# Sigmoid attention into a SwiGLU block on one Trainium2 core: gate and val of the last two batches by seven block products after attention, with weight sums kept in DRAM

## The chip, the core and the metric

The kernel runs on one core of a Trainium2 chip. The metric is the device time of one execution in microseconds (us); of several executions the median is given.

## The reference

Attention with a sigmoid in place of the softmax, and then a feed-forward block with a gated activation. The output of attention, with its heads put side by side, is the feed-forward block's input.

```python
scores = q @ k.T / sqrt(64) - log(448)      # per batch and head: 8 batches, 12 heads, 448 tokens, head size 64
attn   = sigmoid(scores) @ v
x      = attn, heads side by side           # 3584 tokens x 768
g      = x @ w_gate                         # 768 x 1536
out    = (g * sigmoid(g) * (x @ w_val)) @ w_out   # 1536 x 768, float32
```

## The kernel before, in words

**Attention.** One step `i` takes four heads of one batch; three steps make a batch, so there are NQ = 24 steps. SyncE loads q, k and v (`load`, L291), GpSimd casts them (`cast_qk`, `cast_v`), a DMA transpose makes q and k head-size-major (`tr_dma`, L406), TensorE multiplies the scores (`burst`, L417), ScalarE takes the sigmoid (`sig`, L443, tiles `pt`, a ring of 10), TensorE multiplies with v (`pv`, L455), and DVE and ScalarE copy the result out of PSUM as fp16 tiles `xT` (six per batch, 128 model features x 448 tokens, a ring of 14).

**Gate and val, called F1 here.** `f1` (L529) takes one batch and two of the 12 blocks of 128 hidden columns. Gate is 2 x 6 products of 128x128 weights with 448 tokens. Each product is made of four 64x64 quarter matmuls, which run at the same time in four parts of the array (`quarters`, L511, the matmul is L522). ScalarE takes the sigmoid of the gate (L546), DVE multiplies it with the gate out of PSUM (L552), then val follows in the same way and DVE multiplies the two (L559) into `hT`, the hidden tile of a pair of batches.

**The output product, called F2 here.** For two token tiles of 128 `f2_set` (L631) splits the hidden features and the output columns in halves and makes the product with seven block products in place of eight (the Winograd form of Strassen's method). `weight_sums` (L594) makes the four sums of w_out's blocks once, on DVE, and keeps them in staging slots that are free by then (`wsum`, L244). Each set needs sums of hidden tiles on DVE (L661, L664, L667, L734) and sums of results out of PSUM (L687). Two products are issued together as quarters (`f2_pair`, L757, at L522 too); single ones are full-array matmuls (`f2_single`, L788, at L678), which all of the last pair of batches are.

**The order of the work** comes from a planner in the kernel (`list_schedule`, L70). The code from L868 on appends operations, step by step, with a duration, what they depend on, and which buffers they take and give back; the planner goes through time and lets each engine start, out of a window of the next 30 to 40 of its operations, the first one that is ready. The result is a fixed order for each engine's queue; on the chip each engine runs its queue in that order. In before, F1 follows attention at one block per quarter of a step (`LAG`), F2 is added at a rate of 12.5/22 pairs per quarter step, and what is left goes behind. The stores of F2 results are issued on GpSimd's queue during attention and on SyncE's afterwards (L704).

**PSUM** has eight banks, which the planner hands out one by one (`"P": 8`). Staging is 11 slots of 128 x 3.5 KB; from a point on (`uses[1]`) loads use the first five (`NEARLY`) and the others hold weight sums and kept hidden tiles.

Of the kernel before, what the change touches and what calls it, by code (L numbers as in the profile page):

```python
# [11 lines left out]
BF16 = mybir.dt.bfloat16  # L12
COPY = mybir.ActivationFunctionType.Copy
SIGM = mybir.ActivationFunctionType.Sigmoid
MULT = mybir.AluOpType.mult
ADD = mybir.AluOpType.add
SUB = mybir.AluOpType.subtract
# [10 lines left out]
class Op:  # L28
# [3 lines left out]
    def __init__(self, eng, dur, fn, deps=(), mode=("F", "F"), take=(), give=(), desc=(0, 0)):  # L32
        self.eng, self.dur, self.fn, self.mode = eng, dur, fn, mode
        self.deps = [d if isinstance(d, tuple) else (d, 0.0) for d in deps if d is not None]
        self.take = [Slot(t) for t in take]
        self.give = list(give)
        self.rank = self.t0 = self.t1 = None
        self.first = False
        n, size = desc
        self.hold = n == 1792  # L40
        self.dma = 2.0 if n == 1792 else n / 16 * max(0.042, size / 22300 - 0.003)
# [13 lines left out]
LAG = 1  # L55
# [8 lines left out]
TURN = "ACT"  # L64
WO = 4
MARGIN = 1.0
FREE = {"P"}


def list_schedule(ops, bufs, window):  # L70
# [113 lines left out]
def kernel(  # L184
# [30 lines left out]
    ctx.enter_context(tc.manual_schedule())  # L215

    slots = {"A": 2, "P": 8, "st": 11, "src": 2,
             "v16": 3, "qkT": 3, "pt": 10, "xT": 14, "osb": 3, "osf": 4, "S": 2, "t1": 3, "s16": 2}

    idn = one.tile([128, 128], BF16, tag="idn", name="idn")  # L220
    sb_t = one.tile([128, 1], FP32, tag="sbiast", name="sbiast")
# [21 lines left out]

    def wsum(j, c, n=1):  # L244

        x = (j - 1) * NH + c
        o = x % 4 * HW
        return stt[NEARLY + x // 4].bitcast(FP16)[:, o:o + n * HW]

# [10 lines left out]
    def bank(name, n=0):  # L260

        return psum.tile([128, 512], FP32, tag=f"P{R['now'].got('P')[n].n}", bufs=1, name=name)

    def cp(eng, o, i):
        if eng == "ACT":
# [177 lines left out]
    def sig(key, dep, slot):  # L443
        def fn(a):
            def go():
                if a == 0:
                    T[("pt",) + key] = sb.tile([128, 2, S], FP16, tag="pt", bufs=slots["pt"], name="pt")
                nc.scalar.activation(out=T[("pt",) + key][:, a], in_=T[("sc",) + key][a][:, 0:S], func=SIGM, bias=sbias,  # L448
                                     scale=qkscale)
            return go  # L450
        x = op("ACT", 0.44, fn(0), deps=[dep], take=["pt"], give=slot[1:2])
        R["pt ring", key] = x.take
        R["sig"] = R[("pt",) + key] = op("ACT", 0.44, fn(1), deps=[x and (x, LAT["ACT"] + LATE)], give=slot[:1] + slot[2:])

    def pv(i):  # L455

# [72 lines left out]
    def f1(b, f):  # L529

        two = (f, f + 1)
        m, o = divmod(b, 2)

        def both(w, nm, parts, p):
            def fn():
                if p == 0:
                    for n, x in enumerate(two):
                        T[nm, b, x] = bank("ps_" + nm, n)[:, 0:S]
                quarters([[(T[nm, b, x], w[x // FC][:, j, (x % FC) * 128:(x % FC + 1) * 128], T["xT", b, j]) for x in two]
                          for j in range(*parts[p][1:])], parts, p, (nm, b, f))  # L540
            return fn

        def fs(f):
            def fn():
                t = T["s16", b, f] = sb.tile([128, S], FP16, tag="s16", bufs=slots["s16"], name="s16")
                nc.scalar.activation(out=t, in_=T["g", b, f], func=SIGM)  # L546
            return fn

        def ft(f):
            def fn():  # L550
                t = T["t1", b, f] = sb.tile([128, S], FP16, tag="t1", bufs=slots["t1"], name="t1")
                nc.vector.tensor_tensor(out=t, in0=T["g", b, f], in1=T["s16", b, f], op=MULT)  # L552
            return fn

        def fh(f):
            def fn():
                if o == 0 and f == 0:
                    T["hT", m] = sb.tile([128, NF, 2 * S], FP16, tag="hT", bufs=2, name=f"hT_{m}")
                nc.vector.scalar_tensor_tensor(  # L559
                    out=T["hT", m][:, f, o * S:(o + 1) * S], in0=T["v", b, f], scalar=HSC,  # L560
                    in1=T["t1", b, f], op0=MULT, op1=MULT)
            return fn
        xs = [(R["xT", b, j], 0.19 * j) for j in range(KC)]
        old = R["f2", m - 2] if m >= 2 and b % 2 == 0 else []

        def joint(w, nm, deps):
            a = None
            parts = [(0, 0, KC), (1, 0, KC)]
            if (b, f) == (0, 0) and nm in SPLIT:
                parts = [(0, 0, 4), (1, 0, 4), (1, 4, KC), (0, 4, KC)]  # L570
            ws = [(x, 0.38 * n) for c in {x // FC for x in two} for n, x in enumerate(R["w16", "w" + nm, c])]
            for p, (t, j0, j1) in enumerate(parts):
                same = p and parts[p - 1][0] == t
                a = op("PE", 0.19 * (j1 - j0), both(w, nm, parts, p), mode=("Q", "Q"), take=[] if p else ["P", "P"],
                       deps=[(x, 0.19 * n) for n, (x, _) in enumerate(xs[j0:j1])] + deps + ws +
                       [a and ((a, LAT["PE"] + LATE) if same else turn(a, (nm, b, f, p - 1)))])
                banks = banks if p else a.take
            return a, banks
        g, gbank = joint(wg16, "g", [])
        ts = []  # L580
        for n, x in enumerate(two):
            s = op("ACT", 0.45, fs(x), deps=[g], take=["s16"])
            s.first = 2
            ts.append(op("DVE", 0.54, ft(x), deps=[s], take=["t1"], give=s.take + gbank[n:n + 1]))

        def val():
            v, vbank = joint(wv16, "v", old + [(g, 1.0)])
            if f == NF - 2:
                v.give += [x for o, _ in xs for x in o.take]
            for n, (x, t) in enumerate(zip(two, ts)):  # L590
                R["hT", b, x] = op("DVE", 0.54, fh(x), deps=[v, t] + old, give=vbank[n:n + 1] + t.take)
        return val

    def weight_sums():  # L594

# [264 lines left out]
    def f1_step(b, f):  # L860
# [4 lines left out]
        if b % 2 == 1 and f == NF - 1:  # L865
            f2q.extend(f2_items(b // 2))

    f2acc = 0.0  # L868
    wsums = weight_sums()
    next(wsums)  # L870
    fpos = 0
    for i in range(NQ + QB + 2):
        att = i < NQ
        for sl in range(4):
            if i < QB:
                nf = 0
            elif i < QB + 4:
                nf = 1 if sl < 3 else 0
            else:
                nf = min(2, max(0, 4 * (i - QB) + sl - LAG - fpos + 1))  # L880
            if i < NCW and sl == 3:
                cast_wc(i)
            if WO < i <= WO + 4 and sl == 1:
                for f in range(3 * (i - WO - 1), 3 * (i - WO)):
                    cast_wo(f)
            if i > WO + 5 or i == WO + 5 and sl > 1:
                for _ in range(WSN):
                    next(wsums, None)
            f1s = []
            while len(f1s) < nf and fpos < B * NF and ("xT", fpos // NF, KC - 1) in R:  # L890
                f1s.append(divmod(fpos, NF))
                fpos += 1
            later = bursts(i, sl)
            for ds in later[:1 if i >= SPREAD else 2]:
                burst(ds)
            if sl == 0 and QB < i <= NQ:
                pv(i - 1)
            if sl == 0 and 0 < i < QB:
                pv(i - 1)
            if sl == 3 and i == QB - 1:  # L900
                pv(i)
            if att and i + 1 < NPE and sl in (1, 2):
                tr_pe(i + 1, sl - 1)
            for b, f in f1s:
                f1_step(b, f)
            for ds in later[1:] if i >= SPREAD else []:
                burst(ds)
            if att and sl == 0 and i + 2 < NQ:
                casts(i + 2)
            if att and sl == 1 and NPE <= i + 2 < NQ:  # L910
                tr_dma(i + 2)
            if sl == 1:
                if AHEAD <= i + 3 < NQ:
                    loads(i + 3)
                if WO <= i < WO + 4:
                    for f in range(3 * (i - WO), 3 * (i - WO + 1)):
                        load_wo(f)
                    uses[1] = uses[0]
            f2acc = f2acc + 12.5 / 22.0 if f2q else 0.4
            while f2q and f2acc >= f2q[0][0] and ("ws", 4, NH - 2) in R:  # L920
                w, fn = f2q.pop(0)
                f2acc -= w
                fn(not att)
    while fpos < B * NF:
        b, f = divmod(fpos, NF)
        fpos += 1
        f1_step(b, f)
    while f2q:
        f2q.pop(0)[1](True)

    window = {"PE": 40, "ACT": 30, "DVE": 40, "POOL": 8, "SP": 1}
    end = 0.0
# [39 lines left out]
```

## Time and profile before

| | us |
|---|---|
| median of three runs | 410.2 |
| the three runs | 410.2, 406.92, 410.21 |
| span of the profiled execution, first to last instruction | 407.6 |
| TensorE matmuls busy in the span | 400.1 |
| VectorE (DVE) busy | 230.0 |
| ScalarE (ACT) busy | 223.2 |
| GpSimd (POOL) busy | 132.7 |

The profile is of one execution. Its span is the only time that it gives for itself; it lies between the lowest and the middle one of the three runs. Busy time counts a matmul from its start to its modelled end, and matmuls overlap, so that the number says when TensorE had something under way and not how full its array was. "PE" is TensorE's matmul side, "PEld" its weight loads; "L522" is line 522 of the kernel. The granted clock of TensorE was 0.997 on average. The chain of work is followed back from the last instruction: each piece is what released the one after it.

### The profile page before, as it was taken

To read this page: it belongs to the slowest core of one execution; us is meant where nothing else is said; L and a number is where in the kernel's file an instruction comes from. 1 tells how busy PE (TensorE), PEld (TensorE's weight loads), DVE (VectorE), ACT (ScalarE), POOL (GpSimd) and SP (SyncE) were. 2 spreads that over 40 slices of the span, in tenths; PEclk is the share of its full clock that TensorE was granted. 3 is DMA by queue.
4 is the path that set the end of the run, shared out by engine and by line. 5 is a ranking of instruction groups with operands and counts; after the bars stand their busy time and mean duration, and the time that the engine had idled before them with its cause. 6 is when DMAs were issued, how large, how long until landed. Compare 5 with 4: busy or idle time off the path is not lost.

```text
span 407.6 us, 17541 instructions
## 1 busy us (share of the span) xinstructions
PE 400.1 (98%) x7871; PEld 306.8 (75%) x7873; DVE 230.0 (56%) x420; ACT 223.2 (55%) x472; POOL 132.7 (33%) x194
## 2 busy tenths in 40 slices
PE   8999999999999999999999999999999999999995
PEld 3446667668998787665679888889989898997663
DVE  2624544447795467553564664745465656546874
ACT  4997677757767743377647456475474552121100
POOL 1888855656454221522332322422310200000000
PEclk9999999999999999999999999999999999999998
DMA  7999999999676609455665564663500303010335
GB/s 268 380 376 376 376 277 318 304 320 264 184 185 183 160 26 203 139 129 108 209 183 92 172 136 143 177 133 122 124 4 3 80 2 77 7 42 18 101 85 148
DMA packets 64795, 67.58 MB, mean 166 GB/s; under 512 B 35536, under 2 KB 60880, under 8 KB 64720
## 3 DMA queue, kind: packets, MB, share of 16 engines
q1 hardware_dynamic: 62864, 59.78, 51.6%
q0 software_dynamic: 1536, 6.29, 6.0%
q8 instruction: 61, 1.00, 1.0%
q10 hardware_dynamic: 320, 0.39, 0.3%
q14 instruction: 14, 0.11, 0.1%
HBM read 47.19 MB, written 11.01 MB: 143 GB/s over the span
## 4 chain that ended last, share of the span: by engine, by line
PE 95%; ACT 2%; DMA 1%; issue 1%; DVE 0%; ACTq 0%
PE ps_v L522 27%; PE ps_g L522 27%; PE ps_o L522 16%; PE ps_sc L427 8%; PE ps_pv L468 7%; PE ps_o L678 7%; ACT pt L448 2%; PE ps_warm L818 1%; PE ps_tr L384 1%; DMA st<-in_q_dram 1%; DVE st L687 0%; DVE src L268 0%; ACTq L504 0%
## 5 line engine op out<-in xcount | busy, mean ns | idle before, releaser
L448 ACT ACTIVATE pt<-ps_sc 128x448 f16<-128x448 f32 x336 | 162.7, 550 | 77.8 <-PE ps_sc L427 77.3
L522 PE MATMUL ps_v<-xT,wv 64*64 64x448 f16 x2304 | 136.2, 349 | 0.0
L522 PE MATMUL ps_g<-xT,wg 64*64 64x448 f16 x2304 | 134.6, 349 | 0.8 <-issue 0.6
L522 PEld LDWEIGHTS <-wg 64*64 64x64 f16 x2304 | 93.7, 107 | 22.2 <-issue 2.4
L522 PEld LDWEIGHTS <-wv 64*64 64x64 f16 x2304 | 93.2, 107 | 21.2 <-issue 1.4
L552 DVE TENSOR_TENSOR t<-ps_g,s 128x448 f16<-128x448 f32 x96 | 56.5, 618 | 71.6 <-ACT s L546 71.6
L546 ACT ACTIVATE s<-ps_g 128x448 f16<-128x448 f32 x96 | 48.1, 545 | 59.0 <-PE ps_g L522 50.0
L559 DVE SCALAR_TENSOR_TENSOR hT<-ps_v,t 128x448 f16<-128x448 f32 x96 | 55.4, 618 | 43.4 <-PE ps_v L522 26.2
L427 PE MATMUL ps_sc<-qkT 64*64 64x448 bf16 x672 | 77.2, 354 | 0.1
L270 POOL CAST src<-st 128x896 bf16<-128x896 f32 (+1 forms) x43 | 40.8, 951 | 64.5 <-DMA st<-in_q_dram 35.8
L270 POOL CAST v<-st 64x448 f16<-64x448 f32 (+1 forms) x72 | 41.5, 577 | 60.0 <-PE ps_pv L468 42.5
L522 PEld LDWEIGHTS <-hT 64*64 64x64 f16 x1080 | 52.2, 107 | 7.0 <-issue 0.2
L522 PE MATMUL ps_o<-wo,hT 64*64 64x384 f16 x648 | 49.2, 323 | 0.0
L522 PE MATMUL ps_o<-st,s 64*64 64x384 f16 x480 | 45.7, 323 | 0.0
L468 PE MATMUL ps_pv<-pt,v 64*64 64x448 f16 x672 | 45.3, 350 | 0.1
L522 PE MATMUL ps_o<-st,hT 64*64 64x384 f16 x432 | 41.2, 323 | 0.0
L427 PEld LDWEIGHTS <-qkT 64*64 64x64 bf16 x672 | 33.7, 107 | 9.9 <-issue 1.6
L687 DVE SCALAR_TENSOR_TENSOR osb<-ps_o,osb 128x384 f32<-128x384 f32 x63 | 32.9, 550 | 10.4 <-PE ps_o L522 6.6
L268 DVE CAST xT<-ps_pv 128x448 f16<-128x448 f32 x40 | 23.6, 617 | 25.0 <-PE ps_pv L468 25.0
L697 POOL DMA_DIRECT2D out_dram<-osb x32 | 16.7, 526 | 59.0 <-DVE osb L687 59.0
L468 PEld LDWEIGHTS <-v 64*64 64x64 f16 x672 | 26.6, 107 | 9.1 <-issue 2.7
L522 PEld LDWEIGHTS <-s 64*64 64x64 f16 x480 | 29.1, 107 | 3.8 <-issue 0.4
(44 smaller groups left out, 212.8 us busy)
## 6 DMA issues: line engine op xcount, KB each, us to landing
st<-in_q_dram SPq DMA_DIRECT2D x24, 448.0 KB, 5.0
st<-in_v_dram SPq DMA_DIRECT2D x24, 448.0 KB, 6.6
st<-in_k_dram SPq DMA_DIRECT2D x23, 448.0 KB, 5.9
out_dram<-osb POOLq DMA_DIRECT2D x32, 192.0 KB, 3.3
st<-in_moe_w_gate_dram SPq DMA_DIRECT2D x12, 384.0 KB, 8.8
st<-in_moe_w_val_dram SPq DMA_DIRECT2D x12, 384.0 KB, 8.8
st<-in_moe_w_out_dram SPq DMA_DIRECT2D x12, 384.0 KB, 7.6
out_dram<-st SPq DMA_DIRECT2D x16, 192.0 KB, 2.8
```

Source lines behind the costliest of these rows:

```text
L268: nc.vector.tensor_copy(out=o, in_=i)
L270: nc.gpsimd.tensor_copy(out=o, in_=i)
L427: nc.tensor.matmul(out=sc[a][64 * (g ^ a):64 * (g ^ a) + 64, 0:S].rearrange("k (s p) -> k s p", s=NS), lhsT=kT[r, s, 64 * g:64 * g + 64], ...
L448: nc.scalar.activation(out=T[("pt",) + key][:, a], in_=T[("sc",) + key][a][:, 0:S], func=SIGM, bias=sbias, scale=qkscale)
L468: nc.tensor.matmul(out=T["pv", i, a][64 * g:64 * g + 64, :], lhsT=T["v16", i][r, a, s, :], rhs=T["pt", i, s][r, a, :], start=(s == 0), sto ...
L522: mm = nc.tensor.matmul(out=o[cs], lhsT=w[rs, cs], rhs=x[rs], start=p == 0 and k == 0, stop=p == len(parts) - 1 and k == len(steps) - 1)
L546: nc.scalar.activation(out=t, in_=T["g", b, f], func=SIGM)
L552: nc.vector.tensor_tensor(out=t, in0=T["g", b, f], in1=T["s16", b, f], op=MULT)
L559: nc.vector.scalar_tensor_tensor(out=T["hT", m][:, f, o * S:(o + 1) * S], in0=T["v", b, f], scalar=HSC, in1=T["t1", b, f], op0=MULT, op1=MULT)
L678: nc.tensor.matmul(out=T["p", m, k, n], lhsT=lhs()[:, x // 2, x % 2], rhs=rhs(x), start=x == 0, stop=x == NH - 1)
L687: nc.vector.scalar_tensor_tensor(out=c(*dst), in0=T["p", m, k, n], scalar=HREC, in1=c(*other), op0=MULT, op1=ADD)
L697: dma.dma_start(out=out[rows, cols].rearrange("(p s) d -> s p d", s=NS)[s], in_=T[("osb",) + t][64 * x:64 * x + 64, cols])
```

## The change

- **What is made in another way.** Batches 0 to 5 (`NPLAIN`) keep F1 as it was. For batches 6 and 7, `f1_pair` makes gate and val with seven block products. One factor is split into the two batches and the two halves of the 768 features, the other (weights) into those halves and into hidden block `f` and `f + 6`. A set covers one `f` of six, for both batches. Every product is three full-array matmuls of 128x128 weights with 448 tokens, for gate and for val.
- **Chains in PSUM.** Products 1, 6, 7 and 4 accumulate one after the other in one bank; after 1, 6 and 7 ScalarE copies the sum so far out (`snap`) before the next product goes on. Products 2, and 5 then 3, have banks of their own; DVE adds the copies (`add`). The gate's activation is now one Silu on ScalarE (`silu`), where it was a sigmoid and a multiplication. `fin` multiplies gate and val into `hT`. Every Silu depends on all sigmoids before it.
- **Sums of weights.** `f1_sums` makes four differences of weight blocks for each (gate or val, f), 12 pairs, on DVE during attention, from step `TW0` = 13 and every `TSTEP` = 3 quarter steps. They are made in one staging slot and stored in DRAM by a DMA that ScalarE issues one such interval later in the list of operations. The next pair's first difference is planned at the end of that store plus `TTM` = 4.0 us. `wload` loads them back on SyncE's queue after attention, up to five in SBUF at a time.
- **Sums of xT.** 12 operations on DVE once attention has ended, into space of the transposes' source, one new tile and in place.
- **Order and buffers.** The planner's rate of F1 falls to three blocks per step from step 12 on (`F0`, `FR`), that of F2 to 0.4 and later 0.6 pairs per quarter step (`RATE`, `RATE2`). Three F2 pairs go between the early sets (`MIX`), and three are kept behind the last set (`KEEP`). `xT` has 16 tiles, `pt` nine, which are now handed out like PSUM banks. The third sum of w_out's blocks is made in place, which frees the staging slot. The F2 results of batches 4 and 5 are stored by GpSimd's queue after attention as well.

The core of the diff:

```diff
-FREE = {"P"}
+FREE = {"P", "pt", "W"}
+NPLAIN = 6
+RATE = 0.4
+FR = 3.0
+F0 = 9
+XT = 16
+PT = 9
+RATE2 = 0.6
+KEEP = 3
+NEARLY0 = 5
+TW0 = 13
+TSTEP = 3
+TTM = 4.0
+MIX = 3
...
+        if j == 3:
+            return wo16[:, c:c + n, HW:].rearrange("p c d -> p (c d)") if n == 1 else wo16[:, c:c + n, HW:]
...
+    def f1_sums(nm, f):
...
+        last = R.get("TT") or [x for n in range(WO + 7) for x in [R.get(("v16", n))] + R["cq", n] + R["ck", n]]
+        o = [op("DVE", 0.36, fn(0, b[0, 1], b[0, 0]), deps=ws + [(x, -TTM) for x in last], take=[])]
+        o.append(op("DVE", 0.36, fn(1, b[1, 1], lambda: q(0)), deps=[o[0]]))
+        o.append(op("DVE", 0.36, fn(2, b[1, 1], b[0, 1]), deps=[o[1]]))
+        o.append(op("DVE", 0.36, fn(3, b[1, 0], lambda: q(1)), deps=[o[2]]))
+
+        def store():
+            R["TT"] = R["T", nm, f] = [op("ACT", 0.6, lambda: nc.scalar.dma_start(
+                out=tsum[NH * "gv".index(nm) + f], in_=t[0].rearrange("p k j f -> p (k j f)")), deps=[o[3]],
+                desc=(128, 4 * NC * 256))]
+        return store
+
+    def f1_pair(m):
...
+        first = {1: "A", 2: "B", 5: "E"}
+        chain = {1: "A", 6: "A", 7: "A", 4: "A", 2: "B", 5: "E", 3: "E"}
...
+                    for j in range(NC):
+                        nc.tensor.matmul(out=T["fp", key], lhsT=win(nm, f, n)()[:, j], rhs=xin[n](j),
+                                         start=n in first and j == 0, stop=j == NC - 1,
+                                         skip_group_check=n not in first)
...
+            both(1, lambda nm: [last] if last else [R["xT", b1, j] for j in range(KC)])
+            for nm in "gv":
+                snap(nm, 1)
+            both(2)
+            add("g", 0, 0, 2, 1, True)
+            silu(0, 0)
+            both(6, lambda nm: [C[nm, "s", 1]])
+            for nm in "gv":
+                snap(nm, 6)
+            add("v", 0, 0, 2, 1, True)
+            fin(0, 0)
+            both(5)
+            both(7, lambda nm: [C[nm, "s", 6]])
+            for nm in "gv":
+                snap(nm, 7)
+            add("g", 1, 1, 5, 7, False)
+            silu(1, 1)
+            add("v", 1, 1, 5, 7, False)
+            both(4, lambda nm: [C[nm, "s", 7]])
+            silu(1, 0)
+            fin(1, 0)
+            fin(1, 1)
+            both(3, lambda nm: [C[nm, 1, 1]])
+            add("g", 0, 1, 3, 6, True)
+            silu(0, 1)
+            add("v", 0, 1, 3, 6, True)
+            fin(0, 1)
...
-                nf = min(2, max(0, 4 * (i - QB) + sl - LAG - fpos + 1))
+                nf = min(2, max(0, int(4 * min(i - QB, F0) + FR * max(0, i - QB - F0) + (4 if i - QB < F0 else FR) * sl / 4 - LAG) - fpos + 1))
...
+            if i >= TW0 and (4 * i + sl) % TSTEP == 0:
+                if tstores:
+                    tstores.pop()()
+                if tpairs:
+                    tstores.append(f1_sums(*tpairs.pop(0)))
...
-            f2acc = f2acc + 12.5 / 22.0 if f2q else 0.4
-            while f2q and f2acc >= f2q[0][0] and ("ws", 4, NH - 2) in R:
+            f2acc = f2acc + (RATE2 if fpos == NPLAIN * NF else RATE) if f2q else 0.4
+            while len(f2q) > (KEEP if fpos == NPLAIN * NF else 0) and f2acc >= f2q[0][0] and ("ws", 4, NH - 2) in R:
                 w, fn = f2q.pop(0)
                 f2acc -= w
-                fn(not att)
-    while fpos < B * NF:
-        b, f = divmod(fpos, NF)
-        fpos += 1
-        f1_step(b, f)
+                fn(False)
+            if i == NQ and sl == 3:
+                sums, wload, one_set = f1_pair(B // 2 - 1)
+                sums()
+                todo = [(nm, f) for f in range(NH) for nm in "gv"]
+                for x in todo[:5]:
+                    wload(*x)
+                last = None
+                for f in range(NH):
+                    last = one_set(f, last)
+                    for _ in range(min(MIX, len(f2q) - KEEP)):
+                        f2q.pop(0)[1](False)
+                    for x in todo[5 + 2 * f:7 + 2 * f]:
+                        wload(*x)
     while f2q:
-        f2q.pop(0)[1](True)
+        f2q.pop(0)[1](False)
+    for _, fn in f2_items(B // 2 - 1):
+        fn(True)
```

## The prediction, on record before the changed kernel ran

> **What bounds the kernel now.** I read the page's engine rows first, then the chain of work that ended last, then the busy time by stretches.
>
> ```profile
> PE 400.1 (98%) x7871; PEld 306.8 (75%) x7873; DVE 230.0 (56%) x420; ACT 223.2 (55%) x472; POOL 132.7 (33%) x194
> ...
> PE 95%; ACT 2%; DMA 1%; issue 1%; DVE 0%; ACTq 0%
> ```
>
> TensorE is on the chain for 95% of 407.6 us. A busy PE is not by itself a PE at its peak, so the stretches and the pieces of the chain have to say whether it streams without holes.
>
> ```profile
> 36.00:100.00 64.00, 63.35 (x1308) 42.33 (x1300) 32.20 (x56) 44.61 (x94) 41.99 (x56) 1.00 1.09 317
> 100.00:140.00 40.00, 40.00 (x836) 35.31 (x831) 28.31 (x48) 28.61 (x62) 17.02 (x22) 1.00 0.64 168
> 140.00:240.00 100.00, 100.00 (x2206) 75.86 (x2202) 58.07 (x108) 55.16 (x118) 28.04 (x43) 1.00 0.56 140
> 240.00:340.00 100.00, 100.00 (x2216) 89.72 (x2208) 53.91 (x100) 56.19 (x118) 22.47 (x36) 1.00 0.35 92
> 340.00:376.00 36.00, 36.00 (x762) 31.06 (x755) 20.51 (x38) 6.74 (x14) 0.00 (x0) 1.00 0.14 36
> ```
>
> Columns: stretch, length, then PE, PEld, DVE, ACT, POOL busy, granted clock, DMA share, GB/s. From 100 us on PE is never idle and the clock is full. So TensorE time removed after 100 us comes off the end, as long as the new order feeds it as well. DVE and ACT were as much as 71% busy (28.31 and 28.61 of 40) without holding PE.
>
> ```profile
> 371.13 1.14 PE ps_g L522 x24
> 372.26 1.14 PE ps_v L522 x24
> 373.40 1.08 PE ps_o L678 x6
> 374.48 1.26 PE ps_v L522 x24
> 375.74 27.42 PE ps_o L678 x168
> ```
>
> This piece of the chain (start, us, what) has all three TensorE prices. Twenty-four 64x64 matmuls of 448 columns, four at a time, are worth six full-array products: 1.136 us (the differences of the starts), 0.189 us per product. A full-array product of 384 columns takes 27.42/168 = 0.163. And where the two kinds meet, the first group of the new kind takes longer: six full ones take 1.08 instead of 6 x 0.163 = 0.98, the next quarter group 1.26 instead of 1.14. Entering full mode costs 0.10 us, going back 0.12.
>
> **What the change does to TensorE.** Removed: gate and val of two batches, 2 batches x 12 column blocks x 2 x 6 = 288 products, 48 groups x 1.136 = 54.5 us. Added: 6 sets x 7 products x 2 (gate, val) x 3 = 252 full-array matmuls of 448 columns. The trace has none of that shape. By the 384-column row: [...] 0.190 us, 47.9 us in all (0.189 by the quarter row gives 47.7). **Saving: 6.6 us.** All other TensorE work (scores, PV, plain blocks of six batches, all output products) is the same number of the same instructions, only in another order. The order of the first 5,000 of 15,700 instructions is untouched, which is about the first 100 us.
>
> **The switches.** The block products are full-array, the output products of batches 4 and 5 put between them are 64x64 quarters. Counting the built instruction order from the end of attention: 14 runs of quarter pairs alternate with 13 runs of block products, then the final products: 27 changes. Before had three there. 24 more, 12 each way: 12 x 0.10 + 12 x 0.12 = **+2.6 us.** [...]
>
> **Inside a set.** The first product of a chain is read by ScalarE (a snap) while the next ones are to accumulate onto the same bank, so TensorE could wait for ScalarE. Durations: ScalarE 0.545 for 448 columns (L546 row), 0.49 back to back; DVE from PSUM 0.618 (L559 row).
>
> ```profile
> L546 ACT ACTIVATE s<-ps_g 128x448 f16<-128x448 f32 x96 | 48.1, 545 | 59.0 <-PE ps_g L522 50.0
> L559 DVE SCALAR_TENSOR_TENSOR hT<-ps_v,t 128x448 f16<-128x448 f32 x96 | 55.4, 618 | 43.4 <-PE ps_v L522 26.2
> L661 DVE TENSOR_TENSOR s<-hT 128x768 f16<-128x768 f16 x14 | 8.4, 602 | 0.1
> ```
>
> Per set: TensorE 42 x 0.190 = 8.0 us; ScalarE 6 snaps + 4 Silu = 10 x 0.545 = 5.5; DVE 7 PSUM operations x 0.618 + 3 of 448 fp16 columns at 602 x 448/768 = 0.35 = 5.4. Neither engine is the bound. The built order in a set without output products is 2g 1v 2v 6g 5g 6v 5v 7g 7v 1g(next) 4g 4v 3g 3v, at 0.57 each. Tightest waits: 4g needs the snap of 7g, two products (1.14 us) against about 0.1 + 0.545 + 0.1 = 0.75; 3v needs the DVE sum after 7v, four products (2.28) against snap and sums of g and v, about 2.0. Both fit by 0.3 us or more, so I take 0; a miss of 0.5 per set would be 3.0 us. DVE also gets 12 sums of xT (12 x 0.35 = 4.2 us) before the first set's adds, covered by 5.2 us of plain and output products plus the first set's products 1 and 2; 0, at most 1.5 if that cover falls short.
>
> **The table.** Silu after Sigmoid is one table load. The trace has one, 1.283 us (L808). [...] It stands after the snaps of product 6 in the first set; the next snap (7g) is needed after product 7v and half an output pair, about 2.9 us later. By the row 0[...]. I take 0.
>
> **Weight sums.** 48 DVE subtractions of 384 fp16 columns: 0.30 each by the L661 row halved, 0.43 by the dearest (L605 with both inputs from wo, 891/2 = 0.45): 14 to 21 us, spread over nine steps of attention. Per step of 12.5 us (below) DVE then has 3.7 for three column blocks, 1.1 for xT, 2.8 for output sums and 1.9 for these, 9.5 or 76%. The 100-140 stretch ran at 71% with PE full, so 0. ScalarE issues 12 stores of 384 KB: an issue on ScalarE's queue took 0.55 us (L697), 6.6 us over some 130 us, beside 56% of busy time: 0. Each store waits for the last subtraction; sigmoids queue behind it, TensorE has F1 and output products meanwhile. The subtractions of the next pair wait for the store, as they share one buffer; the planner leaves it 7.3 us after issue (its 3.3 for the transfer and TTM 4.0). Stores of 192 KB landed in 2.9 us, so 384 KB should in 3 to 5.3. The loads back (12 x 384 KB, five ahead) run on SP after the last q, k, v load, in a phase where the DMA engines were 14% busy (last stretch shown): 0. If all this cover were gone: 17 + 6.6 us.
>
> **Attention.** Six batches of plain blocks and fewer output pairs per step (0.4 for 0.57) make steps of about 12.5 us: three column blocks 6.8, 1.6 pairs x 1.95 = 3.1, scores and PV 2.6. ScalarE has 14 x 0.49 + 3 x 0.49 + about 1.5 = 9.9 in it, 79%. At 36-100 us it had 44.61 of 64, 70%, with PE at 99%. It should hold, with less room.
>
> **Sum.** -6.6 + 2.6 = -4.0: span 407.6 to 403.6. The runs lie at 406.92, 410.2 and 410.21; the profiled span is 2.6 below their median and above their lowest, so the execution profiled is an ordinary one, and I take the 4.0 off the median: **406.2 us**, 1.0% faster, right at the 1% that a measurement of this kernel can tell from no change.
>
> **Rivals.** *A, the forecast:* switches paid, nothing else. 404.5 to 408.5.
> *B, switches mostly hidden, order as good as planned:* full 6.6 or nearly, 403.6; also reached if fewer TensorE instructions shorten the 2.5 us of issue on the chain. Against it: the 1.08 and 1.26 above. 402.0 to 404.5.
> *C, the saving is eaten by waits in the sets:* 0.3 to 0.8 us per set and at the block's start (DVE runs its 12 sums, output adds and block adds in one order, and the planner reckons 0.54 for what takes 0.618). +2.5 to +4.5: 408.5 to 411, no change.
> *D, slower:* the stores of weight sums land late. The 384 KB weight loads took 8.8 us, when the DMA engines were full. Landing at 8.8 instead of the planned 7.3 holds the DVE queue 1.5 us at each of 11 reuses, and the bank-freeing t, hT and xT behind it; if PE sees half, +8, so 414. It decides from 7.3 us of landing time. Against it: DMA share 0.35 to 0.56 there, and 2.9 us for half the size.
>
> **Chances.** A 50%, B 22%, C 16%, D 12%. Of A, 60% lies below 406.1. Faster by over 1%: 0.22 + 0.30 = 0.52; within 1%: 0.20 + 0.16 = 0.36; slower: 0.12. The range for 8 in 10 takes A, B and C: 402.0 to 411.0; A alone 404.5 to 408.5.
>
> **What would show it.** Right: PE busy about 394 with no wait in its queue over 0.5 us, 252 block matmuls at 0.19 us apart, full groups after quarters 0.1 us longer, attention's last PV near 298 us (403.6 less 48 + 2.6 + 23 + 28 + 4 of block, switches, pairs and plain halves, final products and drain). C: PE or its loads waiting for ACT snaps or DVE sums at the block products. D: DVE waiting for a DMA of the weight-sum store, and store landing over 7 us. B: no lengthening at the mode changes. I am wrong in the main step if the saving on TensorE is not near 6.6, or if TensorE stands during attention.

## The result, and the profile after

| | before | after |
|---|---|---|
| median, first comparison (4 runs each), us | 410.05 | 403.62 |
| lowest to highest, us | 406.92 to 410.21 | 403.15 to 404.99 |
| ratio, 95% interval | | 0.9878 (0.9832 to 0.9923) |
| span of the profiled execution, us | 407.6 | 402.1 |
| TensorE busy, us | 400.1 | 394.9 |

Forecast were 406.2 us and 1.0%; it is 403.6 and, by the ratio, 1.2%. The two medians are 6.4 us apart. Two more comparisons with many more runs of before, each on a chip of its own, give 403.07 against 407.26 (0.9904, 0.9875 to 0.9933) and 403.51 against 407.94 (0.9902, 0.9878 to 0.9926): 4.2 and 4.4 us. So most of what the first shows beyond 4 us belongs to its runs of before; whether to its chip or to the chance of four runs is not shown.

The stretches of the profile after (stretch, length, then PE, PEld, DVE, ACT, POOL busy, granted clock, DMA share, GB/s):

```profile
100.00:140.00 40.00, 40.00 (x840) 32.34 (x836) 27.24 (x49) 28.21 (x61) 17.01 (x23) 1.00 0.70 191
140.00:240.00 100.00, 99.65 (x2185) 81.82 (x2178) 68.05 (x132) 63.33 (x135) 34.75 (x53) 1.00 0.73 200
240.00:290.00 50.00, 50.00 (x1104) 35.44 (x1100) 34.56 (x72) 34.86 (x74) 11.04 (x18) 1.00 0.54 152
290.00:310.00 20.00, 20.00 (x317) 13.84 (x306) 13.18 (x29) 10.24 (x19) 2.83 (x5) 1.00 0.17 44
310.00:330.00 20.00, 20.00 (x289) 10.61 (x288) 14.19 (x30) 7.27 (x14) 2.07 (x4) 1.00 0.38 117
330.00:372.00 42.00, 41.88 (x350) 21.66 (x349) 27.76 (x56) 21.72 (x43) 2.87 (x6) 1.00 0.16 48
```

TensorE stays full but for a few tenths of a microsecond, although DVE and ScalarE are busier than before in the middle (68 and 63 of 100, where before had 58 and 55). The new work on them lies beside TensorE's. The block products run from 299.84 to 366 us; these are pieces of the chain of work there (start, us, what):

```profile
297.89 1.95 PE ps_o L549 x48
299.84 0.67 PE ps_g L727 x3
...
303.43 0.57 PE ps_g L727 x3
...
306.26 0.57 PE ps_v L727 x3
306.83 1.10 PE ps_o L549 x24
307.93 0.67 PE ps_g L727 x3
...
310.31 2.07 PE ps_o L549 x48
312.38 0.68 PE ps_g L727 x3
...
365.99 2.10 PE ps_o L549 x48
368.09 0.02 issue
368.11 0.02 ACTq L531
368.14 0.04 issue
368.18 1.17 PE ps_o L549 x24
369.35 28.39 PE ps_o L903 x174
```

Every product of three matmuls takes 0.567 us (six from 303.43 to 306.83 take 3.40). The first one after output products takes 0.67: entering full mode costs 0.10. Twenty-four quarter matmuls after a product take 1.10 where 0.975 is their price inside a run (48 in 1.95 us, first line): 0.125 for going back. No piece of the chain between the products is a wait for ScalarE or DVE. The last lines show something that the prediction didn't reckon with. A pair of output products is issued in two halves of 24 quarter matmuls, and the second half waits for the first through an empty instruction on ScalarE's queue: the turn (ACTq L531). Where block products or another pair's half stand between, nothing of it is seen. Here three halves stand in one run. The 72 quarter matmuls take 3.36 us from 365.99 to 369.35, where 0.125 and three times 0.975 make 3.05: the turn costs 0.3 us.

### The profile page after: what moved, and what is told of

Same layout as the page of the kernel before. It is cut to its first block, busy times and chain, and to the rows that moved or that the text cites. A ratio compares the mean times of both kernels' runs of the same rounds, so it can differ in the third digit from the quotient of the medians.

```text
span 402.1 us, 15922 instructions
## 1 busy us (share of the span) xinstructions
PE 394.9 (98%) x6973; PEld 270.7 (67%) x6973; DVE 254.2 (63%) x492; ACT 243.6 (61%) x509; POOL 136.2 (34%) x202
## 4 chain that ended last, share of the span: by engine, by line
PE 85%; DMA 11%; POOL 1%; SPq 1%; issue 0%; DVE 0%; POOLq 0%; ACTq 0%
PE ps_v L549 19%; PE ps_g L549 18%; PE ps_o L549 17%; PE ps_o L903 7%; PE ps_sc L452 6%; PE ps_pv L495 6%; DMA st<-in_v_dram 6%; PE ps_g L727 6%; PE ps_v L727 6%; DMA st<-in_moe_w_gate_dram 5%; SPq L325 1%; POOL v L295 1%; POOL wg L366 1%; DVE st L912 0%; POOLq L295 0%
## 5 line engine op out<-in xcount | busy, mean ns | idle before, releaser
L549 PE MATMUL ps_v<-xT,wv 64*64 64x448 f16 x1728 | 103.0, 349 | 0.4 <-issue 0.3
L549 PE MATMUL ps_g<-xT,wg 64*64 64x448 f16 x1728 | 101.7, 349 | 0.3 <-POOL wg L366 0.2
L549 PEld LDWEIGHTS <-wg 64*64 64x64 f16 x1728 | 66.2, 107 | 21.6 <-issue 1.1
L549 PEld LDWEIGHTS <-wv 64*64 64x64 f16 x1728 | 65.7, 107 | 21.1 <-issue 1.9
L579 DVE TENSOR_TENSOR t<-ps_g,s 128x448 f16<-128x448 f32 x72 | 43.1, 620 | 52.1 <-ACT s L573 51.4
L549 PE MATMUL ps_o<-wo,hT 64*64 64x384 f16 x888 | 72.4, 324 | 0.1
L586 DVE SCALAR_TENSOR_TENSOR hT<-ps_v,t 128x448 f16<-128x448 f32 x72 | 41.7, 618 | 23.4 <-PE ps_v L549 22.0
L922 POOL DMA_DIRECT2D out_dram<-osb x40 | 20.8, 525 | 96.4 <-DVE osb L912 96.2
L573 ACT ACTIVATE s<-ps_g 128x448 f16<-128x448 f32 x72 | 37.0, 549 | 23.1 <-PE ps_g L549 13.0
L727 PEld LDWEIGHTS <-st 128*128 128x128 f16 x144 | 13.8, 98 | 13.6 <-issue 1.2
```

Of the source, the lines that this page charges most:

```text
L549: mm = nc.tensor.matmul(out=o[cs], lhsT=w[rs, cs], rhs=x[rs], start=p == 0 and k == 0, stop=p == len(parts) - 1 and k == len(steps) - 1)
L586: nc.vector.scalar_tensor_tensor(out=T["hT", m][:, f, o * S:(o + 1) * S], in0=T["v", b, f], scalar=HSC, in1=T["t1", b, f], op0=MULT, op1=MULT)
L727: nc.tensor.matmul(out=T["fp", key], lhsT=win(nm, f, n)()[:, j], rhs=xin[n](j), start=n in first and j == 0, stop=j == NC - 1, skip_group_ ...
```

## The experiments

Each comparison has its own runs of before. Ratios are to these.

**1. The changed kernel again.** No edit.

> The changed kernel again, unaltered, as the base for the other three on this chip. Theory (6.6 us of products saved, 2.6 paid in mode changes, nothing else after the first 40 us): 1.0 to 1.4% below before. In the profiles the first 36 us differed by 1.7 us although both kernels have the same instructions there; the theory says that this is when the granted clock went to full (9.5 us after the start in the profile of before, 5.9 us in that of after), which belongs to an execution and not to the kernel. So the spans of this kernel should fall on values that differ by about 1.7 us or not at all, and the change's own part is 3.8 us. Rival: the early gain belongs to the change, then it is there in every run.

403.07 us, 0.9904. The profile's span is 401.1. This is the change's size on this chip, 4.2 us, against 4.0 in the prediction's sum.

**2. The products taken out, everything else of the new order kept.**

```diff
-                sums, wload, one_set = f1_pair(B // 2 - 1)
+                for b in (B - 2, B - 1):
+                    for f in range(NF):
+                        f1_step(b, f)
+                        if f % 2:
+                            for _ in range(min(1, len(f2q) - KEEP)):
+                                f2q.pop(0)[1](False)
...
-                if tpairs:
+                if tpairs and False:
```

> The block products and the sums of weights are taken out: batches 6 and 7 get plain gate and val after attention, with the order of attention, rates and buffers of the changed kernel. Theory (the gain is the products alone, the new order brings nothing): the time of before within 0.3% where the clock rises at the same moment, so 4 us slower than after. Rival (the new order of attention is what helps): faster than before by 1 us or more.

Batches 6 and 7 get plain gate and val here, with an output pair after every second block of columns. 407.24 us against 407.26 for before: 1.0000 (0.9984 to 1.0015). The new rates, rings and place of batches 6 and 7 together bring and cost nothing that these runs show. The gain is that of the block products, and it is 4.2 us net.

**3. No output pairs between the sets.**

```diff
-KEEP = 3
+KEEP = 11
-MIX = 3
+MIX = 0
```

> MIX 0 and KEEP 11: the output pairs of batches 4 and 5 are not put between the sets but behind all of them. 5 changes of mode after attention, where after has 27. Theory (each change costs 0.10 to 0.12 us, the waits in a set cost nothing even without pairs between): 22 x 0.11 = 2.4 us faster than after. Rival C (the pairs cover waits of the sets for ScalarE and DVE): the sets now wait 0.3 to 0.8 us each, so the same as after or up to 2 us slower.

404.3 us, 0.9915: not faster than the changed kernel, so by its number rival C. Its profile says otherwise. The chain in the run of pairs behind the sets:

```profile
348.64 2.10 PE ps_o L549 x48
350.75 0.02 issue
350.77 0.02 ACTq L531
350.79 0.04 issue
350.83 2.17 PE ps_o L549 x48
353.01 0.02 issue
353.03 0.02 ACTq L531
353.05 0.04 issue
353.10 2.17 PE ps_o L549 x48
...
370.10 28.40 PE ps_o L903 x174
```

A step from one turn to the next is 353.10 - 350.83 = 2.27 us for 48 quarter matmuls, which take 1.95 when something else stands between the halves. With nothing else to do TensorE loses 0.32 us to the turn through ScalarE at each pair. From 348.64 to 370.10 the run takes 21.46 us for 456 quarter matmuls, which are worth 18.65 (19 times 0.975, and 0.125 for the change of mode): 2.8 us lost in nine turns, where the changed kernel loses 0.3 in one. The sets themselves run at 0.567 per product without a pair between them, but for one place, in the first set on ScalarE and then TensorE:

```profile
304.06 1.28 ACT L766 ACT_TABLE_LOAD   x1
305.36 0.58 ACT L766 ACTIVATE pt<-pt 128x448 f16<-128x448 f32 x1
305.84 0.53 ACT L741 ACTIVATE pt<-ps_v 128x448 f32<-128x448 f32 x1
```

```profile
304.94 0.73 PE L727 MATMUL ps_g<-src,st 128*128 128x448 f16 x3
306.42 0.73 PE L727 MATMUL ps_v<-xT,st 128*128 128x448 f16 x3 [0.75 <-ACT pt L741]
```

Here the table load stands between two snaps, and TensorE waits 0.75 us for the second. So 22 changes of mode are saved, 2.5 us, and 2.5 more in turns and 0.75 are paid: 0.7 us slower by this sum, 0.9 by the two chains from the first block product to the first final product (less the half pair, 0.98 us, that this one has more there), 1.2 by the medians (404.3 against 403.07). Apart from the one wait at the table load, the pairs between the sets do not cover waits of the sets. It is the other way round: the sets cover the pairs' turns.

**4. Block products as quarters,** which takes the mode changes away at their root.

```diff
+                for j in range(NC):
+                    for row in range(2):
+                        nm = two[row ^ p]
+                        rs = slice(64 * row, 64 * row + 64)
+                        for col in range(2):
+                            cs = slice(64 * col, 64 * col + 64)
+                            mm = nc.tensor.matmul(out=T["fp", (nm, f, chain[n])][cs], lhsT=win(nm, f, n)()[:, j][rs, cs], ...
```

> The seven block products are made of 64x64 quarter matmuls, gate and val side by side, each in two halves with a turn between; the order of sets and pairs is the planner's again. No change of mode between sets and pairs (5 after attention). Theory: 2.4 us faster than after, if the turn between two halves finds other work on TensorE; its wait (TensorE to ScalarE and back, some 0.4 us) could cost up to 0.4 x 42 = 17 us where it finds none, so 2.4 faster down to several us slower. Rival (mode changes cost nothing that matters): not faster.

425.13 us, 1.0424: 22 us slower than the changed kernel. There are 42 turns now. Two lines of its waits (who waited for what: us in all, times, longest):

```profile
PEld L800 <- issue: 17.6, 40, 1.0
PE ps_o L935 <- DVE s L921: 3.8, 1, 3.8
```

The weight loads of the products (L800) stand 17.6 us in 40 waits for nothing that the profile names; by their number and place I take these for the turns. TensorE stands 3.8 us for DVE at the end, and the granted clock was 0.95 in the stretch from 370 to 390 us and 0.90 in that from 390 to 424. It gives no price of a mode change; what it points to is the price of the turn without cover.

**5. Sums of weights left out.** The edit keeps the first pair of sums alone and lets all loads read it.

```diff
-    tpairs = [(nm, f) for f in range(NH) for nm in "gv"]
+    tpairs = [("g", 0)]
```

> Left out: the sums of weights of all pairs but the first (44 of 48 subtractions on DVE, 11 of 12 stores); the loads after attention all read the first pair's sums, so gate and val of the last two batches are not the right ones and their time is all that is looked at. Theory (subtractions and stores lie wholly beside TensorE's work): the same time as the changed kernel, within 0.3 us for its part, 403.1 on this chip. Rival D in its mild form (they hold DVE and ScalarE, and TensorE sees some of it): 1 to 3 us faster.

404.33 us, 0.9900 (0.986 to 0.994), the ratio of the changed kernel. In the profile after, the 48 subtractions took 0.40 us each on average, 19.0 in all, the 12 stores 0.33 each on ScalarE's queue. They are hidden, as far as an interval of 1.6 us to either side can tell.

**6. Sums close together.**

```diff
-TSTEP = 3
-TTM = 4.0
+TSTEP = 1
+TTM = 0.0
```

> TSTEP 1 and TTM 0: the pairs of weight sums follow one another closely, each planned for the moment at which the planner takes the store before it as landed (3.3 us after issue; the profile after shows 4.1), so that DVE stands before up to 11 first subtractions for about 0.8 us or more, 9 us in all, with the operations that free PSUM banks behind it. Theory: TensorE has 1 to 2 us of other work at each, so within 1 us of the changed kernel. Rival D: TensorE sees half or more, 4 us or more slower than the changed kernel.

414.55 us, 1.0138 (1.0087 to 1.0189): about 11 us slower than the changed kernel by the medians, 9.5 by the ratios (it has no runs of its own on this chip). The expectation fell, and rival D's mechanism is real, though the changed kernel doesn't suffer from it. A line of this kernel's waits, and a stretch of its chain of work:

```profile
DVE st L643 <- DMA tsum<-st: 9.8, 5, 3.2
```

```profile
140.68 0.28 PE ps_sc L452 x2
140.96 0.07 ACT pt L473
141.02 0.04 issue
141.07 5.92 DMA tsum<-st
146.98 0.02 issue
147.01 0.37 DVE st L643
147.37 0.02 issue
147.40 0.36 DVE st L643
147.75 0.53 DVE t L579
148.29 0.48 DVE osb L912
```

The store of one pair (tsum<-st) takes 5.92 us from its issue, the first subtraction (L643) of the next waits for it in DVE's queue, and behind that stands the gate's multiplication into t (L579), whose bank TensorE waits for (three waits of scores for it, 2.6 us). Five such waits cost DVE 9.8 us, and four stores are on the chain with 5.9 to 6.9 us each. I had thought that TensorE had 1 to 2 us of other work at each; with two operations in a row behind the waiting one, it hasn't. In the profile after the same store landed in 4.1 us (median), and DVE waited for it once, 1.4 us, behind the first store, which took 9.4.

**7. Appended close together, but held 4.0 us after the planned end of the store.**

```diff
-TSTEP = 3
+TSTEP = 1
```

> TSTEP 1 with TTM left at 4.0: the pairs of sums are appended as close together as in the slow close run, but the planner holds each first subtraction until 4.0 us after the planned end of the store. Theory (what cost 11 us there were first subtractions standing in DVE's queue before stores that landed in 6 to 7 us, so the planned distance decides, not the rate of appending): within 1.5 us of the changed kernel. Rival (the load on DVE and ScalarE in a shorter stretch is what cost): 4 us or more slower than the changed kernel.

407.09 us, 0.9963 (0.9946 to 0.9979): between the two expectations, 3.6 us slower than the changed kernel beside it (403.51), 2.5 by the ratios. DVE waits for a store once, 0.8 us. So the planned distance is worth some 7 us of the loss. The rest is lost before the first block product: from there to the first final product it takes as long as the changed kernel (372.52 - 303.02 = 69.50 us and 367.92 - 298.41 = 69.51). It comes with the denser placing, but where it is lost is open. Between 117 and 123 us its chain of work goes over 4.2 us of DVE and 0.6 us of ScalarE pieces, where that of the changed kernel on the same chip has none after 100 us. That is a detour: TensorE's own timeline has it waiting 0.18 us there,

```profile
122.78 0.38 PE L452 MATMUL ps_sc<-qkT 64*64 64x448 bf16 x3 [0.18 <-DVE hT L586]
```

and the chain of experiment 2, which lost nothing, has a like one at 116 us (2.6 of DVE, 0.6 of ScalarE).

**8. Grouped, with both costs of experiment 3 covered.**

```diff
-KEEP = 3
+KEEP = 11
-MIX = 3
+MIX = 0
...
-... for x in [R.get("turn")] if x]))
+... for x in [R.get("turn")] if x and key[0] != 2]))
...
+                op("ACT", 1.5, lambda: nc.scalar.activation(out=warm, in_=sb_t, func=SILU), deps=R["sigmoids"])
                 sums, wload, one_set = f1_pair(B // 2 - 1)
```

> The output pairs of batches 4 and 5 behind the sets, as in the run with MIX 0 and KEEP 11, but without the two costs that its profile shows: a pair no longer waits for the pair before it, so two pairs' halves can alternate and the turn between halves (0.31 us each, 3.1 in all there) has other work beside it; and a one-column Silu right after the last sigmoid loads the table before the first set (2.9 us of TensorE's wait there). Theory (each mode change costs 0.11 us, the sets by themselves wait for nothing): 5 changes in place of 27, 2.4 us faster than the changed kernel. Rival C (sets without pairs between wait): not faster.

One reading in that text was wrong: the 2.9 us at the table load of experiment 3 were a detour of the chain over ScalarE, beside which TensorE went on; it waited 0.75. The result is 401.86 us, 0.984 (0.9804 to 0.9876). On another chip, beside the changed kernel:

> The grouped and covered version again, now on the same chip as the changed kernel. The profiles give from the first block product to the first final product 67.6 us here and 69.5 in the changed kernel, of which one half pair less (0.98) belongs to the place of the first product: 2.8 us less. Theory: 2 to 3 us below the changed kernel, 0.985 of before or less. Rival (the gain on the other chip was its spread): less than 1 us.

401.07 us, 0.9837 (0.9814 to 0.986), against 403.51 and 0.9902 for the changed kernel: 2.4 us faster, and the fastest version here.

> The changed kernel beside the two below: 0.9904 of before again, within 0.3%.

From the chain of the first of these two runs:

```profile
299.51 1.24 PE ps_g L727 x6
...
345.02 4.02 PE ps_o L549 x96
...
351.42 15.72 PE ps_o L549 x384
...
367.14 28.54 PE ps_o L903 x174
```

384 quarter matmuls take 15.72 us, 0.98 per 24: two pairs' halves alternate, and the turn has vanished. From the first block product to the first final one it is 299.51 to 367.14, 67.6 us, with one half pair more in it than the changed kernel's 69.5. So 2.9 us less: 22 changes of mode at 0.115 (2.5) and the turn at the end (0.3) make 2.8.

**9. Before once more.**

> The kernel before once more, for a second profile of it. Theory (1.7 us of the difference between the first two profiles is the moment at which the clock rises, which belongs to the execution): if its clock rises before 6.5 us, the 48 gate matmuls that stood at 36.4 us in the first profile of before stand at 34.5 to 35 us, as in all profiles of changed kernels, and the span is about 405.4. Rival (those 1.7 us are the change's): they stand at 36.4 us again.

The same 48 matmuls in the first profile of before, in this one, and in that of experiment 6:

```profile
36.44 2.44 PE L522 MATMUL ps_g<-xT,wg 64*64 64x448 f16 x48
```

```profile
34.73 2.62 PE L522 MATMUL ps_g<-xT,wg 64*64 64x448 f16 x48
```

```profile
36.74 2.44 PE L549 MATMUL ps_g<-xT,wg 64*64 64x448 f16 x48
```

The span is 405.4 here. The first profile of before was late by 1.7 us at that point and by 2.2 at 104 us, in instructions that both kernels share. Stretches of the start, of the first profile of before, of this one, and of after:

```profile
6.00:8.00 2.00, 2.00 (x14) 0.46 (x13) 0.55 (x3) 0.76 (x2) 0.61 (x1) 1.00 0.98 354
```

```profile
6.00:8.00 2.00, 2.00 (x22) 0.86 (x19) 0.51 (x4) 1.47 (x4) 0.61 (x1) 1.00 1.00 354
```

```profile
6.00:8.00 2.00, 2.00 (x22) 0.84 (x19) 0.51 (x3) 1.53 (x4) 0.49 (x1) 1.00 1.03 370
```

TensorE did 14 matmuls there in the first and 22 in the others. The trace's record of the clock has it at full from 9.5 us after the start in the first profile of before, from 4.6 in the second, from 5.9 in that of after. In experiment 6 it is 10.5, and there the 48 matmuls are late too. The clock column of these lines, 1.00 in all three, doesn't show it.

**10. Longer warm-up.**

```diff
-NWARM = 6
+NWARM = 8
```

> NWARM 8 in place of 6: the warm-up matmuls at the start fill the 0.7 us in which TensorE waits for the first transposes. Theory (the moment at which the clock goes to full, 4.3 to 9.5 us in the profiles so far, [...]the hole at 4.4 us delays it in some executions): the clock rises at 4 to 6 us in each profile, and the time is the same or up to 1 us lower than the changed kernel's, with less spread. Rival (the moment does not depend on the hole): no change in spread or time.

A miss: 403.58 us (402.38 to 406.12), 0.9895, neither faster nor with less spread. Its one profile has the clock at full from 5.5 us; one profile can't tell whether longer warm-up makes an early rise sure.

## Why the prediction was right, point by point

By its level alone the result speaks for another case than the forecast: 403.6 us lies in the band of rival B, where the changes of mode are mostly hidden, and below that of A (404.5 to 408.5). The trace decides for A. Each change of mode shows its 0.10 or 0.125 us on the chain, and the change, 4.2 and 4.4 us with many runs of before, is near A's 4.0 and far from B's 6.6. It is the level of before that was off.

- **The saving on TensorE:** forecast 6.6 us. Measured: 84 products at 0.567 = 47.6 us, so 54.5 - 47.6 = 6.9. The price of one matmul was taken as 0.190 (0.163 x 448/384, from the 384-column row of before); it is 0.189.
- **The changes of mode:** forecast 0.10 and 0.12, 2.6 us for 24, from one lengthened group of each kind in the chain of before. Measured 0.10 and 0.125 in the profile after, 27 changes in its chain as counted, and taken away in experiment 8 they bring what they should (with the turn 2.9 us on the chain, 2.8 by the sum). What happens in TensorE at a change is not shown, only its price.
- **Waits inside the sets:** forecast 0. Right, with and without pairs between them (experiment 3), but for the table load when no pair stands beside it, 0.75 us. In the changed kernel it is covered. In the profile of experiment 3 the load takes 1.28 us and the next activation starts at 305.36, 0.02 us after the load's end, so that the 1.28 of the row was the right price.
- **Weight sums, stores and attention:** forecast 0. Right (experiments 2 and 5), within what their intervals can tell. The last product with v ended at 294.6 us, where some 298 was expected. But the cover is thinner than I argued: rival D's mechanism is real. What keeps it off, by experiments 6 and 7, is the planned distance of 7.3 us from issue to reuse, against a landing of 4.1 us in the median and 9.4 at most; this was tried with the pairs close together, not at the changed kernel's own rate. My price for it (half of DVE's waits seen by TensorE) was too low: from experiment 6 to 7 DVE's waits for stores fall by 9.0 us and the time by some 7.
- **What I did not see:** the turn. 0.3 us are lost at the end of the changed kernel; the sum had no term for it.
- **The level:** the forecast 406.2 is 410.2 less 4.0. The step that failed is that "the execution profiled is an ordinary one". It compared a span with device times. In all 48 later runs of before the device time is 1.95 to 2.07 us longer than the span, so the profiled span of 407.6 stands for about 409.6, beside the two upper runs and not between them and 406.92. Its clock rose late. In the later comparisons the median of before is 407.3 to 407.9 (18 and 19 runs); less 4.0 that makes 403.3 to 403.9, where the changed kernel lies (403.1 to 403.6).
- **The size of the change:** -6.9 for the products, +2.8 for 24 changes of mode at 0.105 and 0.125 and +0.3 for the turn make -3.8 by the pieces of the chain, against -4.2 and -4.4 by the medians. About 0.2 us of the difference lies outside the span: the device time is 2.0 us longer than the span for before and 1.8 for the changed kernel, and also 1.8 in experiment 2, so it comes with the new order and not with the products. By the medians of the spans the change is -4.05 and -4.15. What then is left, 0.2 to 0.3 us, is not settled; it is about the spread of a few runs.

## What to carry to other kernels

When the bound is an engine that never waits, price the removed and added instructions of that engine and every change of its mode at the place where two kinds meet in the trace; here that alone gave the size of the change to 0.6 us (-3.8 against -4.2 and -4.4). Take the level from many runs and compare like with like, spans with spans. Work put between two halves of something that synchronizes, as block products between the halves of a pair, both costs (a change of mode, 0.10 to 0.125 us here) and hides (the wait, 0.32): take it out only together with another cover. A buffer that goes out by DMA and is written again by an engine in the middle of its queue was hidden here with the reuse planned 7.3 us after issue (DVE waited 1.4 us at one store), and not with 3.3 (9.8 us at five); the distance is part of the change, not a detail of it.

## What the runs showed of the hardware that I had not expected

- The moment at which TensorE's clock goes to full differs between executions of nearly the same first instructions. By the record of the clock in the traces it lies at 4.6, 5.5 and 5.9 us after the start in the second profile of before, in experiment 10 and in the profile after, at 9.5 and 10.5 in the first profile of before and in experiment 6. Between the two profiles of before, the late one stands 1.7 us behind by 36 us and 2.2 by 104 us. Why the clock rises late in some executions stays open, and so does whether filling the hole in the warm-up (0.70 us without a matmul before 5.05 us in the first profile of before) makes it sure (experiment 10 has one profile). Of the 11 runs of before beside experiments 5, 6 and 10 seven had spans of 405.0 to 405.4 us and four 407.0 to 409.0; whether the clock rose late in these four is not on record.
- A wait that the chain of work goes through is not all idle time of the bound engine: at the table load the chain left TensorE for 2.9 us, and TensorE stood for 0.75 of them. The engine's own timeline has to be read beside the chain.
